# Batch 1's transposes through the crossbar and q, k staged a batch ahead: sliding-window attention and a hard-swish MoE layer in one kernel

## The chip, the cores and the metric

The kernel runs on one core of one Trainium2 chip. The metric is the device time of one execution in microseconds (us), the median of several runs. In a profile, PE is TensorE, PEld its weight loads, DVE VectorE, ACT ScalarE, POOL GpSimd and SP SyncE; "SPq" is SyncE issuing a transfer, and "L193" is line 193 of that kernel's source. The span is the time from the first to the last instruction of the profiled run; the time is not the same as the span. The granted clock is the share of TensorE's full clock that the profile records.

## The reference, cut to what matters

```python
# q, k, v: (8 batches, 8 heads, 576 tokens, 64); window 128, causal, ALiBi bias
scores = scale * q @ k^T ; scores = where(mask, scores + bias, -1e9)
attn   = softmax(scores) ; o = attn @ v
x      = o.transpose(0, 2, 1, 3).reshape(8*576, 512)
h      = x @ w_in                        # 512 -> 2048
g      = h * clip(h + 3, 0, 6) / 6
out    = g @ w_out                       # 2048 -> 512, float32
```

## The kernel before

All of the attention is interleaved with the MoE matmuls on TensorE. The work comes in 32 groups g of two heads each, four groups (hp = 0 to 3) to a batch b. The loop runs the scores of group g, the exps and masks, the values of group g-1, and between them MoE units of four matmuls (`fill`). Before a batch can be scored its q and k must be cast to bf16 and transposed; after its attention the output must be transposed into `xT` before the MoE may read it.

Two ways of transposing exist. In batches below `NB_PE`, TensorE transposes per pair of heads (`prepare`, `transposes`, and the second half of `back`). From `NB_PE` on, GpSimd casts whole batches and SyncE issues crossbar transposes, which are DMA transfers (`xbar`, and the first half of `back`). Everything that SyncE issues stands in one queue in program order: loads, crossbar transposes of q, k and xT, and outputs.

```python
NB_PE = 2
def load_tokens(b, nm, src):            # five loads of q, k or v of batch b, 256 B runs
    new_load(b, nm)
    for j in range(NQ):
        n = min(128, S - j * 128)
        nc.sync.dma_start(out=ld[b, nm][:n, j, :, :], in_=src[b, :, ds(j * 128, n), :]...)

def xbar(b, nm):                        # q or k of a whole batch, 128 x 2560 bf16
    dst, src = (qTb, qbuf) if nm == "q" else (kTb, kbuf)
    nc.sync.dma_start_transpose(out=dst[b % 2]..., in_=src...)

def by_xbar(g):
    return XBAR_X and NB_PE * NP <= g < G - 1

def back(g):                            # attention output of group g into xT
    if by_xbar(g):
        nc.sync.dma_start_transpose(out=xT[:, hp, ds(b * S, SP)]..., in_=avs...)
        return
    # else: five TensorE transposes and one copy on VectorE

def stage_next(g):                      # called at the end of group g; n = b + 1
    if g == 3:       load_tokens(2, "q", q)
    if g == NP + 1:
        load_tokens(2, "k", k); cast_tokens(2, "q"); xbar(2, "q"); load_tokens(2, "v", v)
    if g == NP + 2:  load_weights_out()            # 2 MB as stored, issued by GpSimd
    # ... (n < NB_PE: return)
    if hp == 0 and n > 2: load_tokens(n, "v", v)
    if hp == 1 and n > 2: cast_tokens(n, "q")
    if hp == 2:
        if n > 2: xbar(n, "q")
        cast_tokens(n, "k"); load_tokens(n + 1, "q", q)
    if hp == 3:
        xbar(n, "k"); cast_tokens(n, "v"); load_tokens(n + 1, "k", k)
# (cut: scores, exps, masks, values, moe_up, moe_down, fill, the loop over groups)
```

`fill` stops when the next MoE unit needs tokens whose `xT` isn't counted as done. A group done by the crossbar counts one group later than one done by TensorE.

The softmax here doesn't subtract the row's maximum and nothing guards it: scores larger than these inputs give would overflow.

Of the kernel before, what the change touches and what calls it, by code (L numbers as in the profile page):

```python
# [18 lines left out]
def kernel(  # L19
# [10 lines left out]
    B, H, S, D = q.shape  # L30
# [5 lines left out]
    NP = H // 2  # L36
# [1 line left out]
    LAST = S - 4 * 128  # L38
    SP = NQ * 128
    W = D + 1  # L40
    NB_PE = 2
    XBAR_X = True
    slopes = [2.0 ** (-8.0 * (h + 1) / H) for h in range(H)]
    n_ms = d_ff // 128
# [3 lines left out]
    G = B * NP  # L48
# [35 lines left out]
    def new_load(b, nm):  # L84
        ld[b, nm] = loads.tile([128, NQ, H, D], FP32, tag="ld", name=f"ld_{nm}")

    def load_pair(b, nm, src, hp):
        t = ld[b, nm]
        for h in (2 * hp, 2 * hp + 1):
            nc.sync.dma_start(out=t[:, 0:4, h, :],  # L90
                              in_=src[b, h, 0:512, :].rearrange("(t p) d -> p t d", p=128))

    def load_tail(b, nm, src):
        nc.sync.dma_start(out=ld[b, nm][:LAST, 4, :, :],
                          in_=src[b, :, 512:S, :].rearrange("h p d -> p h d"))

    def load_tokens(b, nm, src):
# [3 lines that stand above are left out]
            nc.sync.dma_start(out=ld[b, nm][:n, j, :, :],  # L101
                              in_=src[b, :, ds(j * 128, n), :].rearrange("h p d -> p h d"))
# [27 lines left out]
    def load_weights_out():  # L130
        for g in range(4):
            nc.gpsimd.dma_start(
                out=w_out_sb[:, ts(g, 4), :],
                in_=moe_w_out[ds(g * 512, 512), :].rearrange("(m p) d -> p m d", p=128))
# [6 lines left out]
    def cast_tokens(b, nm):  # L141
        s = ld[b, nm]
        if nm == "v":
            for lo in (0, 2):
                nc.gpsimd.tensor_copy(
                    out=vbuf[b % 2][:, lo:lo + 2, :, 0:D].rearrange("p j h d -> p (j h) d"),
                    in_=s[:, lo:lo + 2, :, :].rearrange("p j h d -> p (j h) d"))
            nc.gpsimd.tensor_copy(out=vbuf[b % 2][:LAST, 4, :, 0:D], in_=s[:LAST, 4, :, :])
            return
        dst = qbuf if nm == "q" else kbuf  # L150
        for lo, n, m in ((0, 2, 128), (2, 2, 128), (4, 1, LAST)):
            nc.gpsimd.tensor_copy(
                out=dst[:m, lo:lo + n, :].rearrange("p j c -> p (j c)"),
                in_=s[:m, lo:lo + n, :, :].rearrange("p j h d -> p (j h d)"))

    def xbar(b, nm):
        dst, src = (qTb, qbuf) if nm == "q" else (kTb, kbuf)
        nc.sync.dma_start_transpose(out=dst[b % 2].rearrange("p j h c -> p (j h) c"),
                                    in_=src.rearrange("p j c -> p (j c)"))
# [3 lines left out]
    def prepare(g):  # L163
        b, hp = divmod(g, NP)
        hs = slice(2 * hp, 2 * hp + 2)
        for nm in "qk":
            pr = prs.tile([128, NQ, 2, D], BF16, tag=f"pr{nm}", name="pr")
            t = ld[b, nm]
            nc.vector.tensor_copy(out=pr[:, 0:4, :, :], in_=t[:, 0:4, hs, :])  # L169
            nc.vector.tensor_copy(out=pr[:LAST, 4, :, :], in_=t[:LAST, 4, hs, :])  # L170
            st[g, nm] = pr
        cast_v(b, hs, nc.gpsimd)

    def transposes(g):
        b, hp = divmod(g, NP)
        for nm, dst in (("q", qTb[b % 2]), ("k", kTb[b % 2])):
            src = st.pop((g, nm)).rearrange("p j e d -> p j (e d)")
            tp = ps_h.tile([128, SP], BF16, tag="h", name="tp", padded_shape=[128, 1024])
            for j in range(NQ):
                n = min(128, S - j * 128)  # L180
                nc.tensor.transpose(tp[:, ds(j * 128, n)], src[:n, j, :], ident[:n, :n])  # L181
            eng = nc.vector.tensor_copy if nm == "q" else nc.scalar.copy
            eng(out=dst[:, 0:4, hp, :], in_=tp[:, 0:512].rearrange("p (j c) -> p j c", j=4))
            eng(out=dst[:, 4, hp, 0:LAST], in_=tp[:, 512:S])
# [25 lines left out]
    def exp_diag(g, e):  # L210
        h = 2 * (g % NP) + e
        pd, sc = st[g, "pd"], st[g, "scd"]
        nc.scalar.activation(out=pd[:, e, :, :].rearrange("p j c -> p (j c)"),  # L213
                             in_=sc[:, e, :], func=ACT.Exp,
                             bias=bias_d[:, h:h + 1], scale=scale)
        nc.gpsimd.affine_select(out=pd[:, e, :, :], in_=pd[:, e, :, :],  # L216
                                pattern=[[0, 4], [1, 128]], channel_multiplier=-1, base=0,
                                compare_op=ALU.is_ge, fill=0.0)
# [40 lines left out]
    done = [0]  # L259
# [70 lines left out]
    def fill(n):  # L330
        for _ in range(n):
            if at[0] == len(units):
                return
            nt, fn, step = units[at[0]]
            if fn is moe_up and done[0] < NP * (min((nt * NT + NT - 1) // S, B - 1) + 1):
                return
            fn(nt if fn is moe_up else nt - 1, step)
            at[0] += 1

    src_of = {"q": q, "k": k, "v": v}  # L340

    def stage_next(g):
        b, hp = divmod(g, NP)
        n = b + 1
        if g == 1:
            load_weights_in()
        if g == 2:
            for nm in "qkv":
                new_load(1, nm)
                load_tail(1, nm, src_of[nm])  # L350
                if nm == "q":
                    for i in range(NP):
                        load_pair(1, nm, q, i)
            for i in range(NP):
                load_pair(1, "k", k, i)
                load_pair(1, "v", v, i)
        if g == 3:
            load_tokens(2, "q", q)
        if g == NP + 1:
            load_tokens(2, "k", k)  # L360
            cast_tokens(2, "q")
            xbar(2, "q")
            load_tokens(2, "v", v)
        if g == NP + 2:
            load_weights_out()
        if n < NB_PE or n >= B:
            return
        if hp == 0 and n > 2:
            load_tokens(n, "v", v)
        if hp == 1 and n > 2:  # L370
            cast_tokens(n, "q")
        if hp == 2:
            if n > 2:
                xbar(n, "q")
            cast_tokens(n, "k")
            if n + 1 < B:
                load_tokens(n + 1, "q", q)
        if hp == 3:
            xbar(n, "k")
            cast_tokens(n, "v")  # L380
            if n + 1 < B:
                load_tokens(n + 1, "k", k)

    def segment(lo, hi, fills):
        for g in range(lo, hi + 1):
            f = fills(g)
            if by_xbar(g - 2):
                done[0] = g - 1
            if g + 1 < hi and (g + 1) // NP < NB_PE:
                transposes(g + 1)  # L390
            if g < hi:
                scores(g)
            fill(f[0])
            if g < hi:
                exp_diag(g, 0)
            fill(f[1])
            if g < hi:
                exp_diag(g, 1)
            if g > lo:
                values(g - 1, (0, 1, 2))  # L400
            fill(f[2])
            if g < hi:
                exp_off(g, 0)
            fill(f[3])
            if g < hi:
                exp_off(g, 1)
            if g > lo:
                values(g - 1, (3, 4))
            fill(f[4])
            if g > lo:  # L410
                back(g - 1)
                if not by_xbar(g - 1):
                    done[0] = g
            if g + 2 < hi and (g + 2) // NP < NB_PE:
                prepare(g + 2)
            fill(f[5])
            if g < hi:
                stage_next(g)
            fill(f[6])
# [3 lines left out]
    with tc.manual_schedule(engines=every):  # L423
        for nm in "qkv":
            new_load(0, nm)
        for hp in range(NP):
            for nm in "qkv":
                load_pair(0, nm, src_of[nm], hp)
                if hp == 0:
                    load_tail(0, nm, src_of[nm])  # L430
        constants()
        prepare(0)
        transposes(0)
        prepare(1)
        segment(0, NP, lambda g: (0,) * 7)
        fill(12)
        prepare(NP)
        transposes(NP)
        prepare(NP + 1)
        segment(NP, G, lambda g: (0, 0, 0, 1, 0, 0, 0) if g < 2 * NP else (1, 1, 1, 1, 1, 1, 2))  # L440
        done[0] = G
        fill(len(units))

# [29 lines left out]
```

## Time and profile before

| | before |
|---|---|
| time | 429.94 us (429.66 to 430.02) |
| span of the profiled run | 422.1 us, granted clock 0.919 |
| PE busy | 328.4 us of 422.1 |
| scores wait for the transposed k | 48.8 us in six waits |
| first scores of groups 4, 8, 10, 12, 28, 31 | 54.74, 102.37, 120.52, 143.72, 303.63, 329.55 us |

The last row is read from the timeline of PE, where the first score matmul of each group has its own line.

### The profile page before, as it was taken

Reading aid. Unit: us, or ns where it says so; the run is one execution under the profiler, and the core shown is the slowest. Engines: PE = TensorE matmul, PEld = TensorE weight load, DVE = VectorE, ACT = ScalarE, POOL = GpSimd, SP = SyncE. Lnnn points to the kernel's source line nnn. Section 1 sums busy time; section 2 is a strip of 40 time slices with the busy share of each in tenths; the row PEclk is TensorE's granted clock in tenths of the full one; section 3 lists DMA queues with packets and bytes.
Section 4 is the critical chain, followed back from the end, with each engine's and each line's share of the span. In section 5 each row is a group of like instructions: output and inputs, shape, how many; then the busy total and the mean of one; then the engine's idle time right before and its main releaser. Section 6 shows DMA issues by size and latency. Waiting matters only on the chain.

```text
span 422.1 us, 6554 instructions
## 1 busy us (share of the span) xinstructions
PE 328.4 (78%) x2429; PEld 163.6 (39%) x2429; DVE 173.3 (41%) x376; ACT 202.0 (48%) x373; POOL 147.9 (35%) x245
## 2 busy tenths in 40 slices
PE   1667676302998479859967995899699999999986
PEld 0453243101444244435533452455345444444432
DVE  5544555300554035515532553255255553444311
ACT  2653464402575147627653664466367634434410
POOL 1780047812256136714741454245424300000000
PEclk9999976855899899969996999799899999999999
DMA  8999906999708965997599939895411201010112
GB/s 164 216 193 204 209 1 120 198 204 208 155 17 182 228 150 91 209 219 157 79 207 185 169 90 209 159 168 126 107 40 43 57 32 44 27 49 25 50 51 75
DMA packets 169039, 54.00 MB, mean 128 GB/s; under 512 B 160176, under 2 KB 164528, under 8 KB 169008
## 3 DMA queue, kind: packets, MB, share of 16 engines
q1 hardware_dynamic: 164640, 49.27, 58.6%
q0 software_dynamic: 4224, 4.19, 6.0%
q8 instruction: 19, 0.31, 0.3%
q14 instruction: 12, 0.10, 0.1%
q10 hardware_dynamic: 144, 0.13, 0.1%
HBM read 36.70 MB, written 9.44 MB: 109 GB/s over the span
## 4 chain that ended last, share of the span: by engine, by line
PE 61%; DMA 10%; SPq 10%; DVE 7%; ACT 6%; issue 3%; POOL 3%; POOLq 0%; DVEq 0%
PE hps L284 26%; PE ops L301 24%; DMA kTb<-kbuf 7%; SPq L101 6%; ACT r L288 3%; PE scd L193 3%; DVE g L289 2%; PE av L249 2%; SPq L90 2%; PE av L246 2%; PE sco L200 2%; DVE avs L255 2%; PE tp L181 1%; ACT po L223 1%; POOL pd L216 1%
## 5 line engine op out<-in xcount | busy, mean ns | idle before, releaser
L289 DVE SCALAR_TENSOR_TENSOR g<-r,hps 128x512 bf16<-128x512 f32 x144 | 99.1, 688 | 169.8 <-ACT r L288 169.7
L288 ACT ACTIVATE r<-hps,bias 128x512 f32<-128x512 f32 x144 | 99.5, 691 | 138.5 <-PE hps L284 137.1
L284 PE MATMUL hps<-xT,w_in_sb 128*128 128x512 bf16 x576 | 156.4, 396 | 6.0 <-DVE g L289 3.4
L301 PE MATMUL ops<-w_out_sb,g 128*128 128x512 bf16 x576 | 148.2, 385 | 4.6 <-DVE osb L315 3.9
L301 PEld LDWEIGHTS <-g 128*128 128x128 bf16 x576 | 56.5, 99 | 77.2 <-issue 14.5
L216 POOL TENSOR_SCALAR_AFFINE_SELECT pd<-pd 128x512 bf16<-128x512 bf16 x64 | 39.4, 639 | 129.8 <-ACT pd L213 129.2
L284 PEld LDWEIGHTS <-w_in_sb 128*128 128x128 bf16 x576 | 53.2, 101 | 63.7 <-issue 15.2
L193 PE MATMUL scd<-qTb,kTb 64*128 64x128 bf16 x256 | 15.5, 251 | 48.8 <-DMA kTb<-kbuf 48.8
L213 ACT ACTIVATE pd<-scd,bias_d 128x512 bf16<-128x512 f32 x64 | 40.8, 688 | 26.0 <-PE scd L193 24.7
L228 POOL TENSOR_SCALAR_AFFINE_SELECT po<-po 128x512 bf16<-128x512 bf16 x64 | 41.1, 645 | 27.0 <-ACT po L223 23.8
L223 ACT ACTIVATE po<-sco,bias_o 128x512 bf16<-128x512 f32 x64 | 44.3, 693 | 0.0
L255 DVE TENSOR_TENSOR avs<-av,rc 128x384 bf16<-128x384 f32 x64 | 31.4, 491 | 2.2
L254 DVE RECIPROCAL rc<-av 128x6 f32<-128x6 f32 x64 | 11.8, 185 | 49.1 <-PE av L249 48.9
L193 PEld LDWEIGHTS <-kTb 64*128 64x128 bf16 x256 | 8.9, 107 | 59.4 <-DMA kTb<-kbuf 51.5
L246 PE MATMUL av<-vbuf,po 128*128 128x65 bf16 x256 | 26.8, 204 | 4.8 <-DVE avs L255 4.8
L181 PE MATMUL tp<-ident,pr 128*128 128x128 bf16 (+1 forms) x80 | 10.9, 263 | 19.3 <-DVE pr L169 16.8
L249 PE MATMUL av<-vbuf,pd 128*128 128x65 bf16 x256 | 25.7, 205 | 0.0
L246 PEld LDWEIGHTS <-po 128*128 128x128 bf16 x256 | 21.1, 105 | 10.3 <-DVE avs L255 7.8
L249 PEld LDWEIGHTS <-pd 128*128 128x128 bf16 x256 | 20.7, 104 | 9.9 <-issue 1.6
L313 ACT COPY osb<-ops 128x512 f32<-128x512 f32 x18 | 10.6, 586 | 25.5 <-PE ops L301 25.5
L226 ACT ACTIVATE p4buf<-sco,bias_d 128x64 bf16<-128x64 f32 x64 | 21.0, 328 | 0.0
L181 PEld LDWEIGHTS <-pr 128*128 128x128 bf16 (+1 forms) x80 | 6.3, 113 | 25.2 <-DVE pr L169 20.1
(49 smaller groups left out, 182.3 us busy)
## 6 DMA issues: line engine op xcount, KB each, us to landing
out_dram<-osb SPq DMA_DIRECT2D x35, 256.0 KB, 2.1
ld_q<-in_q_dram SPq DMA_DIRECT2D x24, 256.0 KB, 4.6
ld_k<-in_k_dram SPq DMA_DIRECT2D x24, 256.0 KB, 4.5
ld_v<-in_v_dram SPq DMA_DIRECT2D x24, 256.0 KB, 4.7
ld_q<-in_q_dram SPq DMA_DIRECT2D x24, 128.0 KB, 4.0
ld_k<-in_k_dram SPq DMA_DIRECT2D x24, 128.0 KB, 4.0
ld_v<-in_v_dram SPq DMA_DIRECT2D x24, 128.0 KB, 4.0
w_in_sb<-in_moe_w_in_dram POOLq DMA_DIRECT2D x4, 512.0 KB, 10.1
```

Of the source, the lines that this page charges most:

```text
L193: nc.tensor.matmul(scd[:, e, ts(j, 128)], lhsT=kT[r, j, :], rhs=qT[r, j, :], start=True, stop=True)
L213: nc.scalar.activation(out=pd[:, e, :, :].rearrange("p j c -> p (j c)"), in_=sc[:, e, :], func=ACT.Exp, bias=bias_d[:, h:h + 1], scale=scale)
L216: nc.gpsimd.affine_select(out=pd[:, e, :, :], in_=pd[:, e, :, :], pattern=[[0, 4], [1, 128]], channel_multiplier=-1, base=0, compare_op=AL ...
L223: nc.scalar.activation(out=po[:, e, :, :].rearrange("p j c -> p (j c)"), in_=sc[:, e, :], func=ACT.Exp, bias=bias_o[:, h:h + 1], scale=scale)
L228: nc.gpsimd.affine_select(out=po[:, e, :, :], in_=po[:, e, :, :], pattern=[[0, 4], [-1, 128]], channel_multiplier=1, base=-1, compare_op=A ...
L246: nc.tensor.matmul(av[:, i, e, :], lhsT=po[:, e, qt - 1, :], rhs=vb[:, qt - 1, h, :], start=True, stop=False)
L249: nc.tensor.matmul(av[:, i, e, :], lhsT=d, rhs=vb[:, qt, h, :], start=(qt == 0), stop=True)
L255: nc.vector.tensor_tensor(out=st[g, "avs"][:, qts[0]:qts[0] + nq, :, :], in0=av[:, 0:nq, :, 0:D], in1=rc[:, 0:nq, :, :].to_broadcast([128, ...
L284: nc.tensor.matmul(hps, lhsT=w_in_sb[:, ks, ts(ms, 128)], rhs=xT[:, ks, ts(nt, NT)], start=(ks == 0), stop=(ks == n_ks - 1))
L288: nc.scalar.activation(out=r6, in_=hps, func=ACT.Relu, bias=bias3[:, 0:1], scale=1.0 / 6.0)
L289: nc.vector.scalar_tensor_tensor(out=gts[nt][:, ms, :], in0=r6, scalar=1.0, in1=hps, op0=ALU.min, op1=ALU.mult)
L301: nc.tensor.matmul(ops[nt, sub], lhsT=gts[nt][:, ms, ts(sub, 128)], rhs=w_out_sb[:, ms, :], start=(ms == 0), stop=(ms == n_ms - 1))
```

## The change

It has three main parts. Batch 1 no longer uses TensorE for transposing (`NB_PE` is 1): q, k and the attention output go through GpSimd's casts and the crossbar. The loads, casts and transposes of q and k are moved a batch earlier, so that k's transpose stands in SyncE's queue two to three groups ahead of its use. And in batch 0 the copy of k^T is placed between the exps (a function `first_batch` of its own). Besides, `w_in` is loaded one group earlier, and MoE units are dealt out anew: 7 instead of 12 before group 4, two instead of one in each group of batch 1. Cut to its core:

```diff
-    NB_PE = 2
+    NB_PE = 1
...
-        # staging as shown above
+        if g == 0:
+            load_weights_in()
+        if g == 2:
+            for nm in "qkv":
+                load_tokens(1, nm, src_of[nm])
+        if b == 1:
+            if hp < 3:
+                cast_tokens(2, "qkv"[hp])
+            if hp in (1, 2):
+                xbar(2, "qk"[hp - 1])
+            if hp == 3:
+                load_weights_out()
+        if b >= 2 and b + 1 < B:
+            if hp < 2:
+                xbar(b + 1, "qk"[hp])
+            if hp in (0, 2):
+                cast_tokens(b + 1, "kkv"[hp])
+        if b >= 1 and b + 2 < B:
+            if hp > 0:
+                load_tokens(b + 2, "qkv"[hp - 1], (q, k, v)[hp - 1])
+            if hp == 3:
+                cast_tokens(b + 2, "q")
...
-        prepare(NP); transposes(NP); prepare(NP + 1)          # batch 1 by TensorE
+        first_batch()
+        for nm in "qkv":
+            cast_tokens(1, nm)
+        xbar(1, "q")
+        load_tokens(2, "q", q)
+        xbar(1, "k")
+        load_tokens(2, "k", k)
+        load_tokens(2, "v", v)
+        fill(7)                                               # 12 before
```

More of the change, by code (lines that the diff above doesn't have):

```diff
@@ L340 @@
     src_of = {"q": q, "k": k, "v": v}
+    src_of = {"q": q, "k": k, "v": v}
     def stage_next(g):
         b, hp = divmod(g, NP)
-        n = b + 1
-        if g == 1:
+        if g == 0:
             load_weights_in()
@@ L348, in stage_next @@
             for nm in "qkv":
-                new_load(1, nm)
-                load_tail(1, nm, src_of[nm])
-                if nm == "q":
-                    for i in range(NP):
-                        load_pair(1, nm, q, i)
-            for i in range(NP):
-                load_pair(1, "k", k, i)
-                load_pair(1, "v", v, i)
-        if g == 3:
-            load_tokens(2, "q", q)
-        if g == NP + 1:
-            load_tokens(2, "k", k)
-            cast_tokens(2, "q")
-            xbar(2, "q")
-            load_tokens(2, "v", v)
@@ L364, in stage_next @@
-        if g == NP + 2:
-            load_weights_out()
-        if n < NB_PE or n >= B:
-            return
-        if hp == 0 and n > 2:
-            load_tokens(n, "v", v)
-        if hp == 1 and n > 2:
-            cast_tokens(n, "q")
-        if hp == 2:
-            if n > 2:
-                xbar(n, "q")
-            cast_tokens(n, "k")
-            if n + 1 < B:
-                load_tokens(n + 1, "q", q)
-        if hp == 3:
-            xbar(n, "k")
-            cast_tokens(n, "v")
-            if n + 1 < B:
-                load_tokens(n + 1, "k", k)
+                load_tokens(1, nm, src_of[nm])
@@ new lines, in first_batch @@
+    def first_batch():
+        prepare(0)
+        transposes(0)
+        prepare(1)
+        for g in range(NP + 1):
+            if g < NP:
+                scores(g)
+                exp_diag(g, 0)
+                exp_diag(g, 1)
+            if g + 1 < NP:
+                transposes(g + 1)
+            if g < NP:
+                exp_off(g, 0)
+                exp_off(g, 1)
+            if g > 0:
+                values(g - 1, (0, 1, 2))
+                values(g - 1, (3, 4))
+            if g + 2 < NP:
+                prepare(g + 2)
+            if g > 0:
+                back(g - 1)
+                done[0] = g
+            if g < NP:
+                stage_next(g)
@@ L388, in segment @@
                 done[0] = g - 1
-            if g + 1 < hi and (g + 1) // NP < NB_PE:
-                transposes(g + 1)
             if g < hi:
@@ L413, in segment @@
                     done[0] = g
-            if g + 2 < hi and (g + 2) // NP < NB_PE:
-                prepare(g + 2)
             fill(f[5])
@@ L431 @@
         constants()
-        prepare(0)
-        transposes(0)
-        prepare(1)
-        segment(0, NP, lambda g: (0,) * 7)
-        fill(12)
-        prepare(NP)
-        transposes(NP)
-        prepare(NP + 1)
-        segment(NP, G, lambda g: (0, 0, 0, 1, 0, 0, 0) if g < 2 * NP else (1, 1, 1, 1, 1, 1, 2))
+        first_batch()
[7 more added lines that the diff above has]
+        fill(7)
+        segment(NP, G, lambda g: (0, 1, 0, 1, 0, 0, 0) if g < 2 * NP else (1, 1, 1, 1, 1, 1, 2))
         done[0] = G
```

## The prediction

> **What bounds the kernel now.** I read the page of the kernel before first: the span in 40 slices and the chain that ended last.
>
> ```profile
> PE   1667676302998479859967995899699999999986
> PEclk9999976855899899969996999799899999999999
> DMA  8999906999708965997599939895411201010112
> PE 61%; DMA 10%; SPq 10%; DVE 7%; ACT 6%; issue 3%; POOL 3%; POOLq 0%; DVEq 0%
> PE hps L284 26%; PE ops L301 24%; DMA kTb<-kbuf 7%; SPq L101 6%; ACT r L288 3%; PE scd L193 3%; DVE g L289 2%; PE av L249 2%; SPq L90 2%; PE av L246 2%; PE sco L200 2%; DVE avs L255 2%; PE tp L181 1%; ACT po L223 1%; POOL pd L216 1%
> ```
>
> TensorE (PE) carries 61% of the chain, so the matmuls are the floor: 328.4 of 422.1 us busy. But DMA, and SPq (SyncE issuing transfers), hold 10% each. The PE row dips in slices 7 and 8 (zeros at 77 to 103 us) and then about every fourth slice, and PEclk dips with it. The view of waits says on what:
>
> ```profile
> PE scd L193 <- DMA kTb<-kbuf: 48.8, 6, 21.9
> ```
>
> Six waits, one for each batch 2 to 7, of the first score matmul for the crossbar-transposed k: 48.8 us, the longest 21.9. The chain in order of time shows the longest, and that it is a queue: SyncE issues loads (L101) until 97, and only then the transpose (L158).
>
> ```profile
> 80.31 6.08 SPq L101
> ...
> 97.18 5.14 DMA kTb<-kbuf
> ...
> 102.37 0.61 PE scd L193 x8
> ```
>
> Then stretches of the span (columns: stretch, length, busy us of PE, weight load, VectorE, ScalarE, GpSimd, then granted clock, DMA share, GB/s):
>
> ```profile
> 35.00:50.00 15.00, 12.62 (x47) 4.75 (x46) 7.29 (x12) 7.56 (x11) 1.70 (x4) 1.00 1.13 218
> 53.00:67.00 14.00, 9.19 (x93) 5.12 (x91) 7.31 (x23) 8.95 (x20) 7.79 (x14) 0.76 0.01 2
> 77.00:103.00 26.00, 2.16 (x31) 1.26 (x30) 2.26 (x6) 2.68 (x6) 9.54 (x14) 0.59 1.17 199
> 138.50:142.00 3.50, 0.36 (x2) 0.00 (x0) 0.00 (x0) 0.00 (x0) 0.00 (x0) 1.00 1.21 257
> 185.00:225.00 40.00, 34.00 (x272) 16.96 (x271) 17.02 (x34) 22.63 (x42) 18.55 (x29) 0.93 0.88 163
> 330.00:404.00 74.00, 71.61 (x371) 32.68 (x364) 33.50 (x56) 33.04 (x51) 2.75 (x5) 1.00 0.10 38
> ```
>
> The DMA engines are idle from 53 to 67 (2 GB/s) and saturated from 77 to 103 (199 GB/s, nothing computing): batch 2's loads come too late. In a later batch (185 to 225) PE works 34 of 40 us and stands still in the rest. The tail (330 to 404) is pure MoE, PE at 97%: nothing to win there.
>
> **What the Trainium skill says.** (1) "TensorE: Matmul & The Clock Gate", What's actually happening: after an idle window of about 3.4 us the array runs at half clock until it has been busy about as long. The trace agrees: after the wait that ends at 143.7 the first four MoE matmuls take 1.89 us, four warm ones 0.86. (2) "DMA: Bandwidth & Descriptors", Anatomy of one DMA: a semaphore wait happens on the issuing sequencer, the DMA engines only drain their queues. So a transfer behind a blocked one in SyncE's program waits too, as at 80 to 97 us. (3) Same page, Specifications: line rate needs 512 B or more per transfer. These loads move 64 floats, 256 B, and saturate at 218 GB/s here; 160176 of 169039 packets are under 512 B.
>
> **The change part by part.** Groups are pairs of heads, g = 0 to 31, four to a batch; a MoE unit is 4 matmuls.
>
> *Batch 0.* Scores before 12.69, 16.47, 23.06, 27.37; first MoE matmul 34.68. k^T now goes to ScalarE after the diagonal exps, and the third and fourth casts come earlier: an estimate of 2 to 3 us, so MoE from 32. It is not on the path: group 4 then waits for its k.
>
> *Batch 1.* Removed: 40 PE transposes of q and k with 16 casts and 8 evacuations on VectorE and 8 evacuations (0.59 and 0.22 us) on ScalarE, and 20 PE transposes and 4 copies for xT. Added: 6 GpSimd casts of q and k, 2 big crossbar transposes, 4 for xT. When does group 4 start? Batch 1's loads (3.54 MB) and w_in (2.1 MB as stored) follow batch 0's issues, which end at 16.7; at 200 GB/s that is 28 us, to 45. SyncE then issues q's transpose (3.1), five loads of the next q (4.5) and k's transpose (3.5), landing about 54. Group 4 began at 54.74 before, so **nothing is gained there**; MoE fills only 7 units meanwhile instead of 12. From there ScalarE has four exps (4 x 0.69), two short ones (2 x 0.33) and two relus (2 x 0.69) = 4.8 us a group; GpSimd 4 x 0.64 + 0.29 of masks and 2.6 of casts = 5.5. At 5.5 to 6 us a group, group 8 is reached at 78. Batch 2's q, k, v now load while the DMA was idle before (53 to 67), so its k lies there at about 78 too. Before, scores of group 8 ran at 102.37: **24 us won**.
>
> *Group 8 and 9.* Batch 1's last xT block now comes by crossbar, behind loads of batch 3 in SyncE's queue, and counts as done one group later: group 8 gets 1 MoE unit instead of 3, and I let group 9's MoE wait 5 us for it. I put group 10's scores at 98, before 120.5: **22 us kept**. Units done by then are 24 instead of 27; three move to the tail: 3 x 0.86 = 2.6 us.
>
> *Batches 3 to 7.* k's transpose is issued three groups ahead of its use, so the boundary waits go. Undisturbed, a group takes 8.11 us (xT transposes issued at 159.46 and 167.57), a batch 32.4. Before: groups 10 to 12 took 143.72 - 120.52 = 23.2 us, 7.0 over 2 x 8.11; groups 12 to 28 303.63 - 143.72 = 159.9, 30.1 over 16 x 8.11; group 28 with a cold clock 9.7, 1.6 over. **Sum 38.7 us**: 27.0 of waiting, the rest cold clock and disturbed groups.
>
> Without a new bound: 422.1 - 22 - 38.7 + 2.6 = 364 us of span.
>
> **The rivals.** (a) *DMA becomes the bound.* A batch moves 3.54 MB of loads (16.6 us at 213 GB/s), two transposes of 0.66 MB (5.1 us at 257), four xT of 0.16 MB (2.6) and four outputs (4.0, an estimate): 28.3 us, within 32.4. For: the whole DMA program is now squeezed into fewer us. To the end of batch 2's loads it needs about 73 us (10.6 MB at 210 GB/s, 50.5; w_in 12, from 2.1 MB at 195 and some; four transposes 10), with w_out (12) and batch 3's loads (17) about 104; batch 4's q and k then come at 114 to 124, while PE would want them cast at groups 11 and 12, 107 to 115. Against: after that it gains 4 us a batch. I charge **8 us**; were there no slack in the queue, it could be 25. (b) *SyncE's queue blocks elsewhere.* xT, outputs, transposes and loads are one in-order queue, about 22 us of issuing per batch; if outputs wait behind xT, two output buffers stall the PSUM evacuation. The before kernel shows little of this (PE waits 0.7 us for ScalarE's evacuation between 145 and 330). Were it to happen each batch: 5 to 15 us. (c) *GpSimd*: masks for values now queue behind casts that wait for loads; group 7 has 2.9 + 3.0 (issuing w_out) + 2.6 = 8.5 us there. In 185 to 225 it is busy 18.55 of 40, so only batches 1 and 2 could suffer, a few us. (d) *The loads were hidden anyway and the gain nil*: the 21.9 us wait with PE idle speaks against it.
>
> **Range and chances.** 364 + 8 = 372 us of span. Unprofiled time was 429.94 at a span of 422.1, 7.8 more: **380 us**. Low 366: no DMA lag and a quicker batch 1. High 398: rival (a) in full. All rivals together leave it below 421, so faster by over 2% is 0.97, same 0.02, slower 0.01.
>
> **What would show it.** The wait of the scores for kTb falls from 48.8 us to under 15, nearly all at batch 1. Group 4's scores at 52 to 57; group 8's at 75 to 82. PE without dips from 100 to about 280, at a clock above 0.95, with DMA share there near 1. The xT transposes of steady groups 8.1 us apart. The prediction is wrong if GpSimd or PE wait for ld_q, ld_k or ld_v in batches 3 to 6 (rival a), if PE waits on osb (rival b), or if group 4 starts well after 57, because the queue holds k's first transpose back.

## The result, and the profile after

The changed kernel takes **396.5 us** (median of four runs, 393.65 to 400.16; the slowest counts as slow, over 1.5% above the fastest, and the other three have a median of 395.14), the kernel before 429.86 in the same rounds. The ratio of the fast runs is 0.9202, with a 95% interval of 0.914 to 0.9264: **faster by 8%**. Ratios here are the mean time of one kernel's fast runs over that of the other's fast runs of the same rounds, so not quite the ratio of the medians. The prediction was 380 us with a range of 366 to 398: the direction and the range hold, the centre was 16.5 us too low. The profiled run had a span of 393.4 us.

The span in 40 slices (9.8 us each) and the chain that ended last, of the changed kernel:

```profile
PE   2577407600458989998999899899999999999985
...
PEclk9999957955659999999999999999999999999999
DMA  7999999899994996999699799952121101001012
GB/s 159 219 196 203 200 215 214 153 160 192 202 163 97 223 223 144 205 198 211 148 211 238 131 221 214 220 112 57 48 71 45 46 27 53 28 27 55 27 53 80
...
PE 59%; SPq 20%; DMA 8%; ACT 3%; issue 3%; POOL 3%; DVE 2%; POOLq 0%
```

From slice 12 on (118 us; the first slice is 0) PE has no dip left and its clock is 9 throughout: the waits at the batch boundaries are gone, as intended. But slices 8 to 10 (78 to 108) are still near empty, and SyncE's issuing has grown from 10% to 20% of the chain. The DMA engines are now busy without the hole that they had at 53 to 67.

The view of PE's waits (total us, number, longest):

```profile
PE scd L193 <- DMA kTb<-kbuf: 36.0, 2, 21.7
...
PE hps L284 <- DMA xT<-avs: 8.1, 4, 4.0
```

The scores waited 48.8 us in six places before. The five later waits, one per batch, are gone, but the large one at group 8 is there in nearly its old length (21.7 against 21.9), and a new one of 14.3 us has come at group 4, where batch 1's k now passes through the crossbar. The view of stretches (same columns as in the prediction), first before, then after:

```profile
36.00:125.00 89.00, 50.60 (x408) 25.38 (x406) 35.93 (x77) 39.40 (x75) 35.19 (x57) 0.77 0.81 147
125.00:225.00 100.00, 79.13 (x643) 39.47 (x643) 37.33 (x77) 50.75 (x96) 46.31 (x72) 0.93 0.87 168
```

```profile
36.00:125.00 89.00, 37.93 (x308) 18.24 (x311) 21.81 (x43) 32.31 (x60) 38.47 (x57) 0.73 1.06 178
77.00:103.00 26.00, 3.23 (x36) 1.79 (x34) 2.56 (x6) 3.24 (x7) 10.24 (x15) 0.56 1.18 182
115.00:122.00 7.00, 6.10 (x36) 2.79 (x35) 4.25 (x9) 5.10 (x11) 2.79 (x5) 0.79 0.01 3
185.00:225.00 40.00, 38.00 (x309) 19.27 (x314) 19.82 (x41) 27.31 (x51) 21.26 (x34) 1.00 1.01 186
```

A DMA share of about 1 means that the 16 engines were busy throughout; the view adds up the times of packets, so it also goes above 1. From 185 to 225 PE works 38 of 40 us at full clock where it worked 34 at 0.93. Up to 125 it works *less* than before, 37.9 us against 50.6 of 89, at a DMA that is saturated for most of it. The mean of 1.06 hides one thing: from 115 to 122, just before group 10 starts, the DMA engines are idle (3 GB/s) and PE works off the MoE units that had been held back. So the kernel splits into a start that won nothing and a steady part that won nearly all.

Why the start won nothing is in SyncE's timeline (start, duration, instruction):

```profile
75.42 5.46 SPq L101 DMA_DIRECT2D ld_q<-in_q_dram  x5
80.99 1.23 SPq L268 DMA_TRANSPOSE xT<-avs  x1
82.34 8.49 SPq L158 DMA_TRANSPOSE kTb<-kbuf  x1
90.87 12.11 SPq L101 DMA_DIRECT2D ld_k<-in_k_dram  x5
...
109.28 1.27 SPq L268 DMA_TRANSPOSE xT<-avs  x1
```

and, for the same time, in GpSimd's and in PE's:

```profile
81.67 3.00 POOL L132 DMA_DIRECT2D w_out_sb<-in_moe_w_out_dram  x4
```

```profile
101.09 0.61 PE L193 MATMUL scd<-qTb,kTb 64*128 64x128 bf16 x8 [21.68 <-DMA kTb<-kbuf]
...
113.32 2.29 PE L284 MATMUL hps<-xT,w_in_sb 128*128 128x512 bf16 x5 [4.02 <-DMA xT<-avs]
```

PE is ready for group 8 at 79.4. Batch 2's k stands cast, but its transpose is third in the queue, behind batch 3's q and the xT of group 5, and starts to issue at 82.34, 8.3 us after the cast's end at 74.0. By then GpSimd has put w_out (2 MB as stored) on the DMA engines. Issuing takes 8.49 us instead of the usual 3 to 4, the landing comes 18.7 us after the start, and the scores run at 101.09. Next group 9's MoE needs the last xT of batch 1: that transpose stands behind the loads of batch 3's k (12.11 us of issuing) and v, is issued at 109.28, and PE waits to 113.32. Group 10 starts at 124.20, later than the 120.52 of before.

### The profile page after: what moved, and what is told of

Read it like the earlier page. It is cut to its first block, busy times and chain, and to the rows that moved or that the text cites. A ratio compares the mean times of both kernels' runs of the same rounds, so it can differ in the third digit from the quotient of the medians.

```text
span 393.4 us, 6368 instructions
## 1 busy us (share of the span) xinstructions
PE 311.4 (79%) x2334; PEld 156.3 (40%) x2369; DVE 164.3 (42%) x348; ACT 199.0 (51%) x365; POOL 151.3 (38%) x246
## 2 busy tenths in 40 slices
DMA packets 176718, 55.95 MB, mean 142 GB/s; under 512 B 167856, under 2 KB 172208, under 8 KB 176688
## 3 DMA queue, kind: packets, MB, share of 16 engines
HBM read 36.70 MB, written 9.44 MB: 117 GB/s over the span
## 4 chain that ended last, share of the span: by engine, by line
PE 59%; SPq 20%; DMA 8%; ACT 3%; issue 3%; POOL 3%; DVE 2%; POOLq 0%
PE ops L301 28%; PE hps L284 25%; SPq L101 14%; DMA xT<-avs 4%; SPq L90 3%; DMA ld_v<-in_v_dram 3%; SPq L158 2%; ACT r L288 2%; PE av L249 2%; PE scd L193 2%; DMA ld_q<-in_q_dram 1%; PE av L246 1%; DVE osb L315 1%; DVE g L289 1%; POOL pd L216 1%
## 5 line engine op out<-in xcount | busy, mean ns | idle before, releaser
L284 PE MATMUL hps<-xT,w_in_sb 128*128 128x512 bf16 x552 | 152.4, 393 | 12.5 <-DMA xT<-avs 8.1
L301 PE MATMUL ops<-w_out_sb,g 128*128 128x512 bf16 x565 | 143.6, 379 | 4.4 <-DVE osb L315 3.4
L301 PEld LDWEIGHTS <-g 128*128 128x128 bf16 x576 | 56.2, 98 | 76.4 <-issue 10.3
L284 PEld LDWEIGHTS <-w_in_sb 128*128 128x128 bf16 x576 | 52.4, 100 | 63.9 <-issue 16.8
L213 ACT ACTIVATE pd<-scd,bias_d 128x512 bf16<-128x512 f32 x64 | 41.0, 688 | 18.7 <-PE scd L193 15.5
L193 PE MATMUL scd<-qTb,kTb 64*128 64x128 bf16 x256 | 14.0, 235 | 37.4 <-DMA kTb<-kbuf 36.0
L246 PE MATMUL av<-vbuf,po 128*128 128x65 bf16 x256 | 25.9, 201 | 8.3 <-DVE avs L255 8.3
L193 PEld LDWEIGHTS <-kTb 64*128 64x128 bf16 x256 | 7.9, 100 | 48.8 <-DMA kTb<-kbuf 36.6
L249 PEld LDWEIGHTS <-pd 128*128 128x128 bf16 x256 | 20.6, 103 | 10.3 <-issue 1.1
L152 POOL CAST qbuf<-ld_q 128x1024 bf16<-128x1024 f32 (+1 forms) x21 | 18.1, 903 | 3.7 <-DMA ld_q<-in_q_dram 3.7
L152 POOL CAST kbuf<-ld_k 128x1024 bf16<-128x1024 f32 (+1 forms) x21 | 18.1, 896 | 3.7 <-DMA ld_k<-in_k_dram 3.7
L313 ACT COPY osb<-ops 128x512 f32<-128x512 f32 x18 | 10.5, 586 | 16.7 <-PE ops L301 16.7
L200 PE MATMUL sco<-qTb,kTb 64*128 64x128 bf16 (+1 forms) x256 | 12.9, 226 | 4.4 <-ACT p4buf L226 4.4
```

The lines of the kernel that those rows point to most:

```text
L152: nc.gpsimd.tensor_copy(out=dst[:m, lo:lo + n, :].rearrange("p j c -> p (j c)"), in_=s[:m, lo:lo + n, :, :].rearrange("p j h d -> p (j h d)"))
L213: nc.scalar.activation(out=pd[:, e, :, :].rearrange("p j c -> p (j c)"), in_=sc[:, e, :], func=ACT.Exp, bias=bias_d[:, h:h + 1], scale=scale)
L246: nc.tensor.matmul(av[:, i, e, :], lhsT=po[:, e, qt - 1, :], rhs=vb[:, qt - 1, h, :], start=True, stop=False)
L249: nc.tensor.matmul(av[:, i, e, :], lhsT=d, rhs=vb[:, qt, h, :], start=(qt == 0), stop=True)
L284: nc.tensor.matmul(hps, lhsT=w_in_sb[:, ks, ts(ms, 128)], rhs=xT[:, ks, ts(nt, NT)], start=(ks == 0), stop=(ks == n_ks - 1))
L301: nc.tensor.matmul(ops[nt, sub], lhsT=gts[nt][:, ms, ts(sub, 128)], rhs=w_out_sb[:, ms, :], start=(ms == 0), stop=(ms == n_ms - 1))
```

## The experiments

Two theories stood first. **A**: w_out's load delays k's transpose, and that wait is the lost time. **B**: the DMA engines are saturated up to group 10, and the amount of data to be moved sets when group 10 can start, whatever the order. From the seventh experiment on there is **C**: neither one wait nor the amount, but that what PE needs next, k's transpose and batch 1's xT, passes through SyncE's in-order queue and the saturated DMA engines; to remove one such wait hands the time to the next transfer in the queue, and only taking the need off that path helps. The expectations are quoted. Diffs are against the changed kernel unless stated. In the listed runs here the time is about 1.7 us more than the span. All results were correct except one that was wrong on purpose.

### e1: w_out one group later

```diff
-            if hp == 3:
-                load_weights_out()
+        if g == 8:
+            load_weights_out()
```

> The load of w_out is issued one group later (after group 8's masks instead of before them). Theory A (batch 2's k transpose lands at 101 us because w_out's 2 MB, issued 0.7 us ahead of it, share the DMA engines): the k transpose of batch 2 lands within 6 us of its issue instead of 18.7, group 8's scores move from 101 to about 88, group 10's from 124 to about 112, span about 381. Rival B (the DMA engines are saturated from 0 to 110 us, so order only moves the wait): group 10's scores stay at 118 or later, span above 389.

393.46 us, ratio to before 0.9199 (0.9159 to 0.924). SyncE's timeline:

```profile
82.53 3.19 SPq L158 DMA_TRANSPOSE kTb<-kbuf  x1
...
97.01 5.71 SPq L268 DMA_TRANSPOSE xT<-avs  x1
102.83 9.69 SPq L158 DMA_TRANSPOSE qTb<-qbuf  x1
```

A is right about the wait: without w_out beside it k's transpose issues in 3.19 us, and group 8 starts 5.2 us after it was issued, at 87.78 instead of 101.09. But w_out now meets the xT and q transposes behind it. MoE waits 16.9 us for xT, and group 10 starts at 122.59. **13.3 us were won at group 8 and 1.6 of them were left two groups later.** These 1.6 us are within the scatter: a second profile of the unchanged kernel has group 10 at 122.20 (after again, below). As the explanation of the lost time, A falls.

### e2 and e3: k's transpose ahead of batch 3's loads, and both edits together

```diff
-            if hp in (1, 2):
-                xbar(2, "qk"[hp - 1])
+            if hp == 1:
+                xbar(2, "q")
+                xbar(2, "k")
```

> Batch 2's k transpose is issued right behind its q transpose, ahead of five loads of batch 3 and of w_out; w_out stays where it is. Theory A: it lands at about 81 us, group 8's scores at 81, group 10's at 105 to 108, span about 375 to 378. Rival B: group 8's scores come early but groups 9 and 10 wait for their xT and loads instead; group 10 at 118 or later, span above 388.

> Both of the two edits above. Theory A: k first already removes the wait, so w_out later adds little: group 10 at 103 to 106, span 373 to 377. Rival B: as before, above 388. If w_out then arrives too late for the first down-projection (group 10), PE waits there on it and this run is slower than k first alone.

e2: 394.65 us, ratio 0.9219 (0.9185 to 0.9254); e3, which has e1's edit too: 393.71, ratio 0.92 (0.9164 to 0.9237). Group 8 starts at 82.45 and 81.88, just as one would want. Group 10 starts at 124.65 and 124.21. In e2 w_out meets batch 3's k loads:

```profile
89.22 14.25 SPq L101 DMA_DIRECT2D ld_k<-in_k_dram  x5
```

Meanwhile GpSimd waits for batch 3's q (8.46 and 2.19 us) ahead of group 8's masks in its own order, and PE 17.9 us for the values behind them. In e3 it is the v loads, and batch 1's xT behind them:

```profile
92.66 18.01 SPq L101 DMA_DIRECT2D ld_v<-in_v_dram  x5
```

The longest of PE's waits for xT is then 15.6 us. Three orders, three different longest waits, and one and the same group 10, at 122.6 to 124.7. That looked like B, although the change's own trace speaks against its plain form: 7 of the last 9 us before group 10 pass at an idle DMA.

### e4: the staging ahead alone, batch 1 by TensorE as before

Against the kernel before: `NB_PE` stays 2, and the staging of batches 3 to 7 is the change's.

```diff
-        # hp == 0..3: v, cast q, xbar q / cast k / load q, xbar k / cast v / load k
+        if g == NP + 2: cast_tokens(2, "k"); load_tokens(3, "q", q)
+        if g == NP + 3:
+            xbar(2, "k"); cast_tokens(2, "v")
+            load_tokens(3, "k", k); load_tokens(3, "v", v); cast_tokens(3, "q")
+        # b >= 2: xbar(b+1), casts, load_tokens(b+2) as in the change
```

> The kernel before with only one part of the change: from batch 2 on, q and k are cast and crossbar-transposed a batch ahead; batch 0 and 1 as before. Theory S (all of the measured gain is in the boundaries of batches 3 to 7): as fast as the whole change, span 390 to 398. Rival (batch 1 by crossbar brought some of the gain): 405 to 415.

393.41 us, ratio 0.9191 (0.9152 to 0.923): the same as the whole change (0.9202). PE's wait for k:

```profile
PE scd L193 <- DMA kTb<-kbuf: 22.2, 1, 22.2
```

Only the wait at group 8 is left, as in the change. **Within the noise, the whole gain is that of staging a batch ahead.**

### e6: batch 1's part alone

The change's batches 0 to 2, with the staging of before for batches 3 to 7. One thing differs in batch 2 as well: batch 3's q is now loaded behind k's transpose and not ahead of it. Cut:

```diff
-        if b >= 2 and b + 1 < B: ...      # the change's staging
+        n = b + 1
+        if g == 6: load_tokens(3, "q", q)
+        if g == 7: load_tokens(3, "k", k)
+        if n < 3 or n >= B: return
+        if hp == 0: load_tokens(n, "v", v)
+        if hp == 1: cast_tokens(n, "q")
+        if hp == 2: xbar(n, "q"); cast_tokens(n, "k"); load_tokens(n + 1, "q", q)
+        if hp == 3: xbar(n, "k"); cast_tokens(n, "v"); load_tokens(n + 1, "k", k)
```

> Batches 0 to 2 staged as in the changed kernel, batches 3 to 7 staged as in the kernel before (k transposed just ahead of its use). Theory S (batch 1's part gains nothing by itself): group 10 at 120 to 126, the boundary waits come back, span 418 to 428. If batch 1's part brought something of its own: below 412.

423.36 us, ratio 0.9885 (0.9832 to 0.9938), within 2%. The waits for k are back in all batches:

```profile
PE scd L193 <- DMA kTb<-kbuf: 46.8, 7, 14.7
```

Group 8 starts at 83.81, nearly as early as in e2, and group 10 still only at 119.80, 0.7 us sooner than in the kernel before. Batch 1's part is worth 1% alone and nothing on top of e4.

### e5: a quarter of w_out

```diff
-        for g in range(4):
+        for g in range(1):
...
+        if g == 3:
+            nc.vector.memset(w_out_sb[:, 4:16, :], 0.01)
```

> The changed kernel with only a quarter of w_out loaded, the rest set to a constant: a wrong result on purpose, 3.1 MB less read by the DMA engines before group 10. Theory B (what sets group 10 is the amount that the DMA engines have to move first, whatever the order): group 10's scores move from 124 to 106 to 112, span 375 to 382. If group 10 is set by something else (the chain of masks, xT and MoE), it moves by under 5 us.

386.73 us, ratio 0.9007 (0.8956 to 0.9058); the result is wrong, since most of w_out is missing. This takes away data: 54.38 MB are moved in all instead of 55.95. Group 10 starts at 117.10, 7.1 us sooner. (The expectation's 3.1 MB are what is read, 33.55 instead of 36.70 MB from HBM; the 1.57 MB are what is stored.) The 1.57 MB at the 199 GB/s that the DMA moved from 77 to 103 before come to 7.9 us (an estimate). So the run lies between the two expectations, 12 to 18 us and under 5, and agrees with B in that estimate. It doesn't decide: group 8 starts 7.6 us sooner too (93.47 against 101.09), so a shorter wait at group 8 that carries through would give the same. k's transpose still took 8.00 us to issue and landed 10.3 us after its start, so even a quarter of w_out costs it 5 us.

### e7: batch 1's q, k and xT by TensorE again, the staging kept

GpSimd still casts batch 1 as a whole, but TensorE transposes it; w_out goes to group 5, batch 3's loads to groups 6 and 7, its casts and transposes to groups 9 and 10 (staging cut below).

```diff
     def by_xbar(g):
-        return XBAR_X and NB_PE * NP <= g < G - 1
+        return XBAR_X and 2 * NP <= g < G - 1
...
-        xbar(1, "q"); load_tokens(2, "q", q); xbar(1, "k"); load_tokens(2, "k", k); ...
-        fill(7)
+        for nm in "qkv": load_tokens(2, nm, src_of[nm])
+        fill(5); transposes_tok(1, "q")      # 20 TensorE transposes from qbuf
+        fill(4); transposes_tok(1, "k")
```

> A version meant to beat both: batch 1 cast by GpSimd as after the change, but transposed by TensorE while it is idle, so that SyncE's queue and the DMA engines are rid of two transposes and group 4 needs no transfer after its k; w_out loaded from group 5 on, batch 3's casts later. Theory B: group 4's scores at 46 to 50 instead of 59, group 8's at 70 to 78, group 12's at 120 to 128 instead of 140, span 372 to 380. If the DMA amount is not the bound, group 12 stays above 135.

381.25 us, ratio 0.8887 (0.8845 to 0.8929). Group 10 starts at 104.05, **20.1 us sooner than in the change**. Group 12 (122.31) and the span (379.4) lie where B had put them, groups 4 and 8 (54.41, 85.80) later than that. It moves 1.95 MB less, because the crossbar's transposes of batch 1 count as DMA traffic; at 200 GB/s that is an estimated 10 us. Half of the gain could be the amount, then, but not all. That needed a cleaner test (e11, below).

### e8: loads one group earlier in the steady batches

The change's groups 12, 17, 21 and 25 take 9.35 to 9.96 us instead of 8.12, 6.0 us over in all: batch b's last xT stands behind batch b+2's v loads in SyncE's queue.

```diff
-            if hp > 0:
-                load_tokens(b + 2, "qkv"[hp - 1], (q, k, v)[hp - 1])
+            i = hp if b > 1 else hp - 1
+            if 0 <= i < 3:
+                load_tokens(b + 2, "qkv"[i], (q, k, v)[i])
```

> From batch 2 on, each load is issued one group earlier, so that no load stands ahead of a batch's last xT transpose in SyncE's queue. If that queue place causes the 1.5 us lost at groups 16, 20, 24 (9.4 to 10.0 us instead of 8.1), those groups take 8.1 to 8.5 us and the span falls by 4 to 5 us, to about 389; if it is only the saturated DMA engines, nothing changes (within 1.5 us).

391.54 us, ratio 0.9135 (0.9083 to 0.9186). Groups 17, 21 and 25 now take 8.48, 8.12 and 8.12 us instead of 9.96, 9.64 and 9.35, so 4.2 us are saved in size as expected (the expectation named the groups before). The start was 3 us later in this profile, so the span of 392.1 doesn't show it; the ratios, 0.9135 against 0.9202, overlap. The expected span of about 389 was missed. The place is shown, its worth in the total is not settled by this run.

### e9, after again, and e10: a kernel out of what was learnt

e9 is e7 with k's TensorE transposes directly behind q's, batch 2's casts and transposes at groups 5 and 6, w_out at group 7, loads a group earlier in the later batches, and one more MoE unit a group in batch 1. e10 differs from e9 in the order of one stretch of SyncE's queue:

```diff
-        if g == 9:
+        if g == 10:                       # now behind batch 3's k transpose
             load_tokens(4, "q", q)
             load_tokens(4, "k", k)
-        if g == 10:
+        if g == 12:
             load_tokens(4, "v", v)
+        if g == 13: load_tokens(5, "q", q)
+        if g == 14: load_tokens(5, "k", k); load_tokens(5, "v", v)
```

> The version with batch 1 transposed by TensorE, with three more edits: k's PE transposes before the second stretch of MoE units, w_out two groups later, and from batch 2 on each load a group earlier. If the DMA engines are the bound up to group 12 (theory B), group 4's scores come at 46 to 48 instead of 54, but group 12's by at most 6 us earlier (116 to 122), and the rest comes from the boundaries: groups 13, 16, 20, 24 take 8.1 to 8.6 us instead of 9 to 17, span 362 to 370. If group 4's start is what carries through, group 12 is at 114 or earlier.

> The changed kernel once more, on the same chip as the version above and beside the same runs of the kernel before: 393 to 399 us; group 8's scores wait for kTb for 18 to 24 us again if that wait is no accident of one run.

> As the tuned version, but batch 3's k transpose stands ahead of batch 4's ten loads in SyncE's queue, and batch 4's v is loaded at group 12. If queue order made group 12 wait 12 us there, group 12's scores come at 110 to 114 instead of 124 and the span falls to 364 to 369. If the DMA engines' amount is the bound (theory B), the wait only turns up again within the next groups (on batch 3's xT, on batch 4's casts or on its transposes): group 16 stays within 3 us of its 153 to 162 in the tuned version, and the span stays at 373 or above.

e9: 376.97 us, ratio 0.8822 (0.8749 to 0.8896). Group 11 starts at 101.94, but group 12 only at 123.77, because batch 3's k transpose stood behind ten loads of batch 4:

```profile
118.67 3.59 SPq L158 DMA_TRANSPOSE kTb<-kbuf  x1
```

PE waited 12.0 us for it. Group 4 came as expected (47.97), but group 12 lies outside both expectations, and so does the span of 376.2. The changed kernel itself, run again beside e9, gave 395.03 us and a ratio of 0.9232 (0.915 to 0.9314), with the wait at group 8 again at 19.7 us: its start is no chance of one run.

e10 moves nothing but those loads: **371.28 us (370.98 to 373.57), ratio 0.8678 (0.8633 to 0.8722)**, faster than both kernels. Group 12 starts at 111.39, as expected for queue order, and group 16 at 153.52, 8.1 us sooner than in e9, where B had allowed 3. The span of 369.7 is just above the 364 to 369 expected: of the 12.4 us won at group 12, 4.3 were gone by group 14, before which PE waits 6.0 and 2.4 us for xT. The stretches of e10, and its wait for k:

```profile
36.00:125.00 89.00, 65.43 (x570) 32.94 (x576) 36.84 (x78) 49.63 (x96) 54.44 (x81) 0.93 1.10 200
125.00:225.00 100.00, 95.47 (x770) 47.90 (x782) 48.40 (x98) 65.63 (x122) 51.47 (x81) 0.96 1.10 209
```

```profile
PE scd L193 <- DMA kTb<-kbuf: 2.0, 2, 1.1
```

PE works 65.4 us of the first 89, against 37.9 in the change, at a DMA as saturated as there (share 1.10 against 1.06). A saturated DMA alone doesn't keep PE from working.

### e11: only the xT of batch 1 by TensorE

This is e3 with one line changed, so that q and k of batch 1 stay with the crossbar:

```diff
     def by_xbar(g):
-        return XBAR_X and NB_PE * NP <= g < G - 1
+        return XBAR_X and 2 * NP <= g < G - 1
```

> The changed kernel with w_out a group later and k(2) ahead of q(3)'s loads, as in e3_both, and besides batch 1's attention output transposed by TensorE instead of the crossbar; batch 1's q and k stay with the crossbar. Theory C (what TensorE needs next stands in SyncE's queue; only taking the need off that queue helps): group 9's MoE no longer waits for an xT transpose (15.6 us in e3_both), group 10 begins at 108 us or earlier against 124.2, and the span is 384 us or less. Theory B (the amount of DMA data sets when group 10 begins): the data moved hardly differ from e3_both, so group 10 begins at 118 us or later and the span is 390 us or more. Between the two would mean that the weights' or batch 3's landing takes the place of part of the wait.

385.6 us (384.24 to 387.12), ratio 0.9018 (0.8964 to 0.9073), span 383.8. Group 10 starts at 104.81, against 124.21 in e3: **19.4 us sooner for 0.65 MB less** (55.30 against 55.95 MB), which at this run's 195 GB/s is an estimated 3.3 us. The line also lets xT count as done a group earlier, so group 8 gets its MoE units back. That can't be the gain: by the loop's counts it puts 27 units instead of 24 before group 10. B falls: the amount isn't what held group 10. C holds for what PE waits for next, and the run shows it a second time, one batch later. C's "only taking the need off that path helps" is too strong, though: e10 gained 8.1 us at group 16 over e9 by order alone. How much of a wait is the queue and how much the full DMA engines, C doesn't say. The start of group 10 and PE's waits, first in e3, then in e11:

```profile
124.21 0.40 PE L193 MATMUL scd<-qTb,kTb 64*128 64x128 bf16 x8
PE hps L284 <- DMA xT<-avs: 25.0, 5, 15.6
PE scd L193 <- DMA kTb<-kbuf: 16.4, 2, 14.6
```

```profile
104.81 0.40 PE L193 MATMUL scd<-qTb,kTb 64*128 64x128 bf16 x8
PE scd L193 <- DMA kTb<-kbuf: 14.6, 1, 14.6
PE hps L284 <- DMA xT<-avs: 12.4, 5, 6.9
```

The one wait for k in e11 is at group 4, where batch 1's k still passes through the crossbar. The 6.9 us wait comes between groups 13 and 14: batch 2's last xT, still by crossbar, is issued at 136.83 behind the v loads of batch 4. Group 12 started 16.9 us sooner than in e3 (123.49 against 140.43), group 14 only 8.1 (149.89 against 157.99). That is where half of the gain went, and why 19.4 us at group 10 became 9.1 in the span.

## Why the prediction was right or wrong

The start times of four groups split the span into the terms of the prediction's sum (us):

| term | predicted | before to after | measured |
|---|---|---|---|
| start to group 10 | -22 | 120.52 to 124.20 | **+3.7** |
| group 10 to group 31 | -38.7 | 209.03 to 176.32 | -32.7 |
| group 31 to the end | +2.6 | 92.55 to 92.88 | +0.3 |
| rival (a), DMA lag, charged whole | +8 | within the first term | |
| change of the span | -50.1 | 422.1 to 393.4 | -28.7 |

The missed 21.4 us of span are 25.7 in the first term, 6.0 in the second, -2.3 in the third, less the 8 that had been charged for the lag. In time the miss is 16.5, because the step from span to time was over-sized as well: 7.8 us in the prediction, taken from a profiled run that was a quick one for that kernel (423.8 of 430), against 3.1 (396.5 less 393.4). That the range holds is in part luck: 396.5 lies near its upper end of 398, which stood for rival (a) in full, and that is not where the time was lost.

1. **The step that failed** is "group 8 is reached at 78. Batch 2's q, k, v now load while the DMA was idle before (53 to 67), so its k lies there at about 78 too ... **24 us won**". PE was there at 79.4, which looks right but is two errors that cancel: group 4 began 5.3 us late, and the groups then took 5.0 us each instead of 6. The second half took *loaded* for *transposed*. k's transpose was third in SyncE's queue, issued at 82.34, and landed 18.7 us later beside w_out, so group 8 started at 101.09, where 1.3 us were won instead of 24. e1 and e3 split this: without w_out beside it group 8 starts at 87.78, with k's transpose moved ahead as well at 81.88, so 13.3 us were the shared DMA engines and 5.9 the place in the queue. The kernel before already showed the first: w_out is issued there at 75.70, and five loads of v and five of q, issued from 75.32 and 86.50 on, held SyncE for 11.06 and 10.56 us, where five such loads at 67.08 had taken 4.16. The prediction had w_out's 12 us in its sum of DMA work, but only to ask when batch 4's data come.
2. **"I let group 9's MoE wait 5 us for it. I put group 10's scores at 98."** The wait was 4.0 us, so the size was right, but group 10 came 26 us after 98, on top of the late group 8. e1, e3 and e11 show that this wait was the next in line: with k sooner, MoE waits up to 16.9 and 15.6 us for xT, and only with xT off the queue does group 10 start at 104.81. So mending the failed step alone would not have made the prediction true.
3. **Batch 1, "nothing is gained there"**: group 4 was put at about 54 and began at 59.32, because k's transpose was issued at 53.73 and landed 5.5 us later. Here a sum was wrong: the prediction's own terms, 45 + 3.1 + 4.5, put the issue at 52.6, and with the 5.1 us from issue to landing that it had read at 97.18 k lands at 57.7, not "about 54". Its sign of being wrong, "group 4 starts well after 57", came true: 4.6 us were lost against 54.74. e10, with both by TensorE, starts group 4 at 47.65.
4. **Batches 3 to 7, 38.7 us**: right in mechanism, 32.7 in size. Steady groups take 8.11 us as foretold (the sign named for it, the xT transposes, are issued at uneven distances of 7.1 to 9.9 us), PE's clock is 1.00 from 145 on, and GpSimd holds nothing up. The missing 6.0 us are groups 12, 17, 21 and 25, which take 1.2 to 1.9 us more than 8.11: rival (b), another transfer held back in the queue, is real, but as an xT behind v loads and not as an output. e8 shows it by taking 4.2 of them away. The queue had less slack than "about 22 us of issuing per batch" made it seem: SyncE's issues from 208.69 to 248.03 before add up to 27.4 us, and those of one batch after, from 148.11 to 183.29, to 30.5.
5. **"Three move to the tail"**: they didn't. Units of the third MoE tile may start only when batch 2's xT is done, so both kernels stand at unit 48 at the end of group 12: the three units that the kernel before had ahead run into this limit. The tail is 0.3 us longer, not 2.6.
6. **Rival (a)** was looked for in batches 3 to 6, where its sign doesn't occur: no wait for ld_q, ld_k or ld_v is listed for PE or GpSimd from 124 to 300. What the DMA cost came in batches 1 and 2. Saturated DMA was right (share 1.16 from 36 to 115), but e10 at 1.10 shows that it needn't stop PE.
7. **"Falls from 48.8 us to under 15, nearly all at batch 1"**: 36.0 us. The four waits of batches 4 to 7 and that of batch 3 went as foretold; 14.3 us are at batch 1 and 21.7 at batch 2.
8. **Smaller slips.** Batch 0's 2 to 3 us didn't come: the first MoE matmul ran at 35.40 after and 34.68 before. In rival (a), 73 + 12 + 17 is 102, not 104. And 0.86 us for four warm matmuls is the distance of starts; the profile's row for four warm ones reads 1.02 to 1.03 beside the cold 1.89.

The skill's part in this: what the prediction drew from "DMA: Bandwidth & Descriptors", Anatomy of one DMA (a transfer behind a blocked one in SyncE's program waits too) was part of the miss, and was applied to the kernel before only, not to the changed queue. Even there the trace shows less than that: from 80 to 97 the transfers ahead weren't blocked by a semaphore, they were issued slowly. The Trainium skill, same page, "Issuing engines are not separate DMA queues", states that transfers of all issuing engines end up on the same 16 DMA engines and interleave there. The trace agrees, 8.49 us of issuing for k's transpose beside w_out from GpSimd, 3.19 without; reading it with the order of issues would have put w_out beside k's transpose in the prediction.

**What stays open.** How the DMA engines divide their time between GpSimd's and SyncE's transfers was not measured: with none, a quarter and all of w_out beside it, k landed 5.2, 10.3 and 18.7 us after its issue began, which is no more than three points; a second profile of the changed kernel gave 17.5 with all of it. How a second issuing engine for the transposes would do was not tried. And how far e10 is from the limit that its saturated DMA sets is not known; batches up to 225 us run at 200 to 209 GB/s there.

## What to carry to other kernels

When a transfer that PE needs is moved earlier in the program, list the whole in-order queue of its issuer at that time, and the other issuers' transfers beside it: data that lie loaded are not data that lie transposed. In a stretch where the DMA is saturated, removing one wait on a transfer mostly hands the time to the next one, so measure at a milestone behind the stretch and not at the wait; what helped here was to do the urgent transposes on an idle TensorE (20 blocks of k in 2.5 us) and to order what was left by when it is needed. And take the step from profile span to time from several runs, not from one profiled run.

## What the Trainium skill lacked or had wrong

- "DMA: Bandwidth & Descriptors", Issuing engines are not separate DMA queues, calls the sequencer's time to start a transfer "usually small relative to the DMA itself". Here it isn't: a crossbar transpose of 128 x 2560 bf16 held SyncE for 3.0 to 4.7 us of the 5.2 us (median) to its landing, and while 2 MB of weights loaded beside it for 8.49 (11.22 in e11); five loads of 256 KB or less held it for 4.2 to 6.2 us, and for 10.5 to 18 beside w_out. The page has no figure for issuing when the DMA engines are full.
- "VectorE: DVE Perf Modes", The three transpose paths, sets 390 ns on TensorE against 1309 ns on the crossbar for one 128 x 128 block. Beyond the crossbar's share of DMA bandwidth it doesn't say what a batch of blocks costs: 20 blocks of k took TensorE 0.22 us each and 2.5 us from the first to the scores that use them, the crossbar 5.2 us undisturbed and 18.7 beside a weight load. So in these runs TensorE's advantage was larger where the DMA was loaded.
- "DMA: Bandwidth & Descriptors", Specifications, gives 512 B as the least run for line rate, but no rate below it; the page's Why small descriptors are slow has an overhead for 256 B, no measured rate. Loads in runs of 256 B, mixed with transposes, kept the engines full at 200 to 209 GB/s for 190 us (e10).
